# Two layers of long convolution and squared-ReLU MLP on one core: three kinds of DMA move to other places in SyncE's queue

## The chip, the core and the metric

The kernel runs on one core of a Trainium2 chip. The core has five engines with a queue of instructions each, worked off in order: TensorE (PE, with its weight loads shown as PEld), VectorE (DVE), ScalarE (ACT), GpSimd (POOL) and SyncE (SP). They tell each other through semaphores when a result is ready. SP computes nothing. It issues the kernel's DMAs, some 2,200 of them, in the order in which the program lists them, and an issue whose wait is not over holds up all that stand behind it. The metric is the device time of one execution in microseconds (us); lower is better.

## The reference, cut to what matters

With S = 2048 tokens, D = 1024 channels and F = 3584, two pairs of layers run one after the other:

```
x = x + A(layernorm(x));  x = x + B(layernorm(x))      # and both once more
A(q):  ks = short causal depthwise convolution of k (4 taps)
       kv = ks * v
       y  = causal convolution of kv with a filter as long as the sequence, per channel
       return q * (y + kv * ssm_D)
B(x):  r = max(x @ w1 + b1, 0);  return (r * r) @ w2 + b2
```

The convolution's result y does not depend on x, so it is computed once and used in both layers.

## The kernel before, in words

The MLP is the main work. The tokens are cut into 4 blocks of 512, and seven units (layer, block) run in turn; every matmul product is made of three passes (`mm3`, lines 355 to 358), since each operand is split into a high and a low part. A unit is a list of steps. A step takes one weight tile (`whl`, a high and a low half) and runs 12 matmuls of 512 columns. At the head of each step, `w_advance` issues the DMA of a weight tile 8 steps ahead into a raw buffer `wr` (lines 1099 and 1102), lets ACT make its high half (L1112) and DVE its low half (L1120). After the step's matmuls `w_store` writes some of the split weights to DRAM (L1128).

The convolution is laid between these steps. Channels are cut into 8 columns `c` of 128, and for each of the later token blocks `sb` = 1, 2, 3 three streams run:

- `fwd_x` (line 374) makes spectra of k*v: it loads `kT` and `vT` (L376, L378), forms the short convolution on ACT and DVE (L383, L386), multiplies by v (L388), transposes on PE (L441), transforms on PE (L412), adds on DVE (L423 to L428) and stores three tiles to `XD` (L433).
- `fwd_g` (line 450) makes spectra of the filter: it loads raw rows (L448) and the half that was carried over from the block before (`KD`, L457), transforms on PE (L475), copies on ACT (L480), combines on DVE (L485 to L490), stores the half to be carried (`KD`, L484), builds three tiles `go[1]`, `go[2]`, `go[0]` on DVE (L504, L505), one tick apart, and stores them to `GD` (L514). These tiles come from a ring of three buffers named `fg`, so the next column's raw rows take the place of `go[1]`. The two PSUM banks named `pt` are used by both streams and by the inverse transform (L616).
- `prod_stream` (line 540) multiplies the spectra. Its units (sb, group of 64 channels, one of three spectra pairs) are numbered 0 to 143, 48 for each sb and 6 for each column. A unit loads a tile from `XD` and one from `GD` (`load`, line 637: `cx` and `cg`, both on L646), POOL multiplies twice (L546), DVE sums each product two ticks later (L550), POOL folds (L696 to L701), PE transforms back (L616), ACT evicts (L622), SP stores to `YD` (L627).

A "tick" is one call of a stream's generator or one turn of a list of things due (`Later`). Several ticks can fall in one step. In sb = 1 a `cx` or `cg` tile holds two neighbouring units, two such tiles exist of each, and `fill` (line 649) calls for more loads after the second product of a unit: after an odd unit n for units n + 2 and n + 3, after the first unit of a column for the next two. Unit n is multiplied two ticks after its loads were called for, or later. With `sb` = 1 the stream often waits for the forward streams, and it catches up at one unit (two products) per step. The list that belongs to the steps (`slag`, among it L627 and the adds of L1729) is turned at a step's start, before `w_advance`; the products run after the step's matmuls, the forward streams behind them. So within one step SP gets, in this order: stores of L627, a weight load, a weight store, spectra loads, then the forward streams' DMAs.

Of the kernel before, what the change touches and what calls it, by code (L numbers as in the profile page):

```python
# [23 lines left out]
NB = S // T  # L24
# [4 lines left out]
BL = 256  # L29
NBL = S // BL  # L30
BT = T // BL
# [220 lines left out]
def tile_h3_mlp(ctx: ExitStack, tc: tile.TileContext, q, kT, vT, shk, ssmT, ssmD, w1, b1, w2, b2,  # L252
                fwd_t, pro_t, inv_t, sgn_t, out):
    nc = tc.nc
    V, A, G, PE, SY = nc.vector, nc.scalar, nc.gpsimd, nc.tensor, nc.sync
# [13 lines left out]
    KD = [[dram.tile([P, 2, BT * P], F32, name=f"kd{sb}_{c}") for c in range(KT)] for sb in range(NB - 1)]  # L269
# [14 lines left out]
    def mkfg(shape, dt=F32):  # L284
        return cv.tile(shape, dt, name="fg", bufs=3)

    def mkfk(shape, dt=F32):
        return cv.tile(shape, dt, name="fk", bufs=2)
# [62 lines left out]
    def give(*tiles):  # L351
        for o in tiles:
            held[slot.pop(id(o))[0]] = False

    def mm3(o, lh, ll, rh, rl, start, stop):
        PE.matmul(o, lh, rh, start=start, stop=False)  # L356
        PE.matmul(o, lh, rl, start=False, stop=False)  # L357
        PE.matmul(o, ll, rh, start=False, stop=stop)  # L358

    def hold(n):  # L360
        got = take(n)
        while not got:
            yield
            got = take(n)
        return got

    def dview(t, sb, c):
        return t[2 * c:2 * c + 2, :, BT * sb:BT * sb + BT].rearrange("g p b u -> p g b u")
# [77 lines left out]
    def load_g(raw, sb, c):  # L446
        for e in range(2):
            SY.dma_start(raw.rearrange("p (e b c) -> p e b c", e=2, b=BT)[:, e], g_rows(sb, c)[:, e])  # L448

    def fwd_g(sb, c):  # L450
        yield
        yield
        raw = mkfg([P, T])
        load_g(raw, sb, c)
        kk = [mkfk([P, 3 * BL]) for _ in range(2)]
        for r in range(2):
            SY.dma_start(kk[r][:, 0:BL], KD[sb - 1][c][:, r])  # L457
        for _ in range(FWD_WAIT):
            yield
        if sb > PLAIN:  # L460
            hi = mkfg([P, T], F32R)
            lo = mkfg([P, T], F32R)
            A.copy(hi, raw)
            yield
            V.tensor_sub(lo, raw, hi.bitcast(F32))
            yield
            yield
            yield
        oa = yield from hold(2)
        for r in range(2):  # L470
            ob = oa[r].rearrange("p (b e c) -> p e b c", b=BT, e=2)
            for e in range(2):
                q_ = slice(e * 256, e * 256 + 256)
                if sb <= PLAIN:
                    PE.matmul(ob[:, e], plain[0][:, 2 * e + r], raw[:, q_], start=True, stop=True)  # L475
                else:
                    mm3(ob[:, e], fh[:, 2 * e + r], fl[:, 2 * e + r], hi[:, q_], lo[:, q_], True, True)
        yield
        for r in range(2):
            A.copy(kk[r][:, BL:], oa[r])  # L480
        yield
        if sb < NB - 1:
            for r in range(2):
                SY.dma_start(KD[sb][c][:, r], kk[r][:, BT * BL:])  # L484
        V.scalar_tensor_tensor(kk[1][:, 0:T], kk[1][:, 0:T], sgn[:, 1:2], oa[0], op0=OP.mult, op1=OP.add)  # L485
        V.scalar_tensor_tensor(oa[1], kk[0][:, 0:T], sgn[:, 0:1], oa[1], op0=OP.mult, op1=OP.add)
        yield
        k0 = kk[1][:, 0:T]
        V.scalar_tensor_tensor(oa[0], oa[1], -1.0, k0, op0=OP.mult, op1=OP.subtract)
        V.tensor_sub(oa[1], oa[1], k0)  # L490
        yield
        odd = mkfg([P, T])
        parts = [t.rearrange("p (b e n) -> p e b n", b=BT, e=2) for t in (k0, oa[1], oa[0])]
        odds = [parts[0][:, 1]]
        for i in range(2):
            odds.append(odd[:, i * BL:i * BL + BL].rearrange("p (b n) -> p b n", b=BT))
            A.copy(odds[-1], parts[i + 1][:, 1])
        yield
        go = [None] * 3
        for i in (1, 2, 0):  # L500
            go[i] = mkfg([P, T])
            u = go[i].rearrange("p (g b u c) -> p u b g c", g=2, b=BT, u=2)
            ev, ov = (t.rearrange("p b (g c) -> p b g c", g=2) for t in (parts[i][:, 0], odds[i]))
            V.tensor_add(u[:, 0], ev, ov)  # L504
            V.tensor_sub(u[:, 1], ev, ov)  # L505
            yield
        if sb <= PLAIN:
            yield
            yield
        give(*oa)  # L510
        yield
        yield
        for i in range(3):
            SY.dma_start(dview(GD[i], sb, c), go[i].rearrange("p (g b u) -> p g b u", g=2, b=BT))  # L514
        yield

    plag, slag = Later(), Later()
    fwd_done = set()
# [2 lines left out]
    def fwd_stream(kind, fwd):  # L521
        for sb in range(1, NB):
            if sb > PLAIN:
                const_split()
            for c in range(KT):
                yield from fwd(sb, c)
                half_done[kind].add((sb, c))
                if all((sb, c) in d for d in half_done.values()):
                    plag.at(3, fwd_done.add, (sb, c))

    streams = [fwd_stream("x", fwd_x), fwd_stream("g", fwd_g)]

    def fwd_tick():
# [6 lines left out]
    def prod_stream():  # L540
        lag = plag
        sums, inv = [0, 0], [0, 0]

        def mult(st, xt, gt, j):
            pr = cv.tile([P, CU, j + 1], F32, name="cp", bufs=3)
            G.tensor_mul(pr.rearrange("p c i -> p i c"), xt[:, 0:j + 1], gt[:, j::-1])  # L546
            st["pr"] = pr
# [86 lines left out]
        got, when = {}, {}  # L634
        share = {}

        def load(n):
            sb, g, ty = units[n]
            nb = BT * sb + BT
            two = nb <= NBL // 2  # L640
            if n % 2 == 0 or not two:
                for nm in ("cx", "cg"):
                    share[nm] = cv.tile([P, 2 if two else 1, nb, CU], F32, name=nm, bufs=2)
            got[n] = [share[nm][:, n % 2 if two else 0] for nm in ("cx", "cg")]
            for t, src in zip(got[n], (XD[PAIRS[ty][0]], GD[PAIRS[ty][1]])):
                SY.dma_start(t, src[g, :, :nb])  # L646
            when[n] = lag.n

        def fill(n):
            sb = units[n][0]  # L650
            room = 3 if BT * sb + BT <= NBL // 2 and n % 2 else 2
            for m in range(n + 1, min(n + room + 1, len(units))):
                if m not in when:
                    if (units[m][0], units[m][1] // 2) not in fwd_done or (m > n + 2 and units[m][0] != sb):
                        return
                    load(m)

        pair = sm = None
        for n, (sb, g, ty) in enumerate(units):
            while n not in when:  # L660
                if (sb, g // 2) in fwd_done:
                    load(n)
                else:
                    lag.tick()
                    yield None
            while lag.n < when[n] + 2:
                lag.tick()
                yield None
            if ty == 0:
                while sums[0] - sums[1] >= 2:  # L670
                    lag.tick()
                    yield None
                sums[0] += 1
                sm = cv.tile([P, 3, BT, CU], F32, name="sm", bufs=2)
                if g % 2 == 0:
                    pair = {}
            for jj in range(BT):
                j = BT * sb + jj
                st = {"pair": pair}
                mult(st, *got[n], j)  # L680
                lag.at(2, red, st, sm, ty, jj)
                if jj == BT - 1:
                    if ty == 2:
                        lag.at(3, fin, st, sm, sb, g, 0)
                    fill(n)
                lag.tick()
                yield (j + 1) * CU * 1e-3
# [905 lines left out]
    lag = slag  # L1593
    xT = first_block()
    pds = prod_stream()
    ml = shut.enter_context(tc.tile_pool(name="ml", bufs=1, reuse_waits="tile"))
    def relu2(st, k):
# [544 lines left out]
    for sb in range(1, NB):  # L2142
        if WIN[sb] > lo_u:
# [3 lines left out]
            n = sum(last_step[u] + 1 - start_step[u] - 19 * (1 - PREP_PACE) for u in range(lo_u, hi_u))  # L2147
# [17 lines left out]
    for s, (k, u, c, a, i, tts, w) in enumerate(steps):  # L2165
# [79 lines left out]
        else:  # L2245
# [4 lines left out]
            r = rs[c, i]  # L2250
# [35 lines left out]
        if u + 1 < NU and not direct[u]:  # L2286
            n = s - start_step[u]
# [89 lines left out]
```

## Time and profile before

| what | us |
|---|---|
| median of 3 runs | 2678.66 (2674.75, 2678.66, 2678.91) |
| the profiled execution | 2673.35 |
| its span, first to last instruction | 2671.6 |
| PE busy | 2622.0 (98%) |
| DVE busy | 1977.1 (74%) |
| ACT busy | 1132.0 (42%) |
| POOL busy | 1044.2 (39%) |

"Busy" is the time in which an engine executes; issuing DMAs and waiting is not counted. The profile also gives the clock granted to TensorE in each stretch as a share of full speed, the chain of waits that ended last, the waits of each engine by what ended them, and a timeline of each engine.

### The profile page before, as it was taken

To read this page: it belongs to the slowest core of one execution; us is meant where nothing else is said; L and a number is where in the kernel's file an instruction comes from. 1 tells how busy PE (TensorE), PEld (TensorE's weight loads), DVE (VectorE), ACT (ScalarE), POOL (GpSimd) and SP (SyncE) were. 2 spreads that over 40 slices of the span, in tenths; PEclk is the share of its full clock that TensorE was granted. 3 is DMA by queue.
4 is the path that set the end of the run, shared out by engine and by line. 5 is a ranking of instruction groups with operands and counts; after the bars stand their busy time and mean duration, and the time that the engine had idled before them with its cause. 6 is when DMAs were issued, how large, how long until landed. Compare 5 with 4: busy or idle time off the path is not lost.

```text
span 2671.6 us, 36107 instructions
## 1 busy us (share of the span) xinstructions
PE 2622.0 (98%) x12388; PEld 2198.9 (82%) x12388; DVE 1977.1 (74%) x2845; ACT 1132.0 (42%) x1929; POOL 1044.2 (39%) x688
## 2 busy tenths in 40 slices
PE   8899999899999999999999999999999999999999
PEld 7888787788888888888888888888788778888887
DVE  7879888789887877779777765456778768777553
ACT  4454344434444333343333422345444575454442
POOL 2536665255642645427554275000100217536111
PEclk9999999999999999999999999999999999999999
DMA  8799898689989899788987888689888898878653
GB/s 253 245 322 316 296 309 280 229 298 377 344 294 318 313 337 302 268 304 302 339 303 251 307 293 301 209 260 320 305 298 304 268 332 256 265 249 312 233 195 119
DMA packets 380265, 763.16 MB, mean 286 GB/s; under 512 B 44064, under 2 KB 159408, under 8 KB 377008
## 3 DMA queue, kind: packets, MB, share of 16 engines
q1 hardware_dynamic: 380080, 760.85, 83.4%
q8 instruction: 98, 1.61, 0.2%
q14 instruction: 87, 0.71, 0.1%
HBM read 583.49 MB, written 177.21 MB: 285 GB/s over the span
## 4 chain that ended last, share of the span: by engine, by line
PE 83%; DMA 7%; DVE 5%; ACT 1%; issue 1%; POOL 1%; SPq 1%; DVEq 0%; ACTq 0%; POOLq 0%
PE p L356 24%; PE p L358 24%; PE p L357 24%; PE pt L356 2%; PE pt L358 2%; PE pt L357 2%; DMA whl<-wd_m 2%; PE p L1195 2%; DMA wr<-w 1%; DVE whl L1120 1%; DMA cg<-gd 1%; PE pt L475 0%; DMA yt<-yd 0%; PE pt L616 0%; PE pt L412 0%
## 5 line engine op out<-in xcount | busy, mean ns | idle before, releaser
L546 POOL TENSOR_TENSOR cp<-cx,cg 128x384 f32<-128x384 f32 (+5 forms) x288 | 542.2, 1896 | 566.2 <-DVE sm L550 371.0
L356 PE MATMUL p<-xh,whl 128*128 128x512 f32 (+1 forms) x1504 | 577.4, 384 | 3.1 <-DMA whl<-wd_m 2.2
L358 PE MATMUL p<-xh,whl 128*128 128x512 f32 (+1 forms) x1504 | 573.4, 381 | 3.3 <-DVE whl L1120 2.8
L357 PE MATMUL p<-xl,whl 128*128 128x512 f32 (+1 forms) x1504 | 573.2, 381 | 0.4 <-DVE xl L1517 0.4
L1112 ACT CAST whl<-wr 128x512 fp32r<-128x512 f32 x546 | 332.3, 619 | 467.8 <-PE p L358 282.2
L1120 DVE TENSOR_TENSOR whl<-wr,whl 128x512 fp32r<-128x512 f32 x486 | 427.6, 891 | 132.0 <-ACT whl L1112 131.0
L356 PE MATMUL p<-whl,rh 128*128 128x512 f32 x1204 | 476.0, 395 | 5.1 <-DVE fg L1718 2.9
L357 PE MATMUL p<-whl,rh 128*128 128x512 f32 x1204 | 471.1, 391 | 2.0 <-POOL whl L1120 1.2
L358 PE MATMUL p<-whl,rl 128*128 128x512 f32 x1204 | 470.6, 391 | 0.0
L358 PEld LDWEIGHTS p<-xh,whl 128*128 128x128 f32 x1504 | 283.7, 189 | 58.2 <-DVE whl L1120 3.0
L356 PEld LDWEIGHTS p<-xh,whl 128*128 128x128 f32 x1504 | 284.0, 189 | 57.6 <-issue 2.2
L357 PEld LDWEIGHTS p<-xl,whl 128*128 128x128 f32 x1504 | 283.8, 189 | 52.7 <-DVE xl L1517 0.6
L1609 DVE TENSOR_TENSOR rl<-wr,rh 128x512 fp32r<-128x512 f32 x140 | 143.0, 1022 | 179.2 <-ACT rh L1606 179.2
L1120 POOL TENSOR_TENSOR whl<-wr,whl 128x512 fp32r<-128x512 f32 x60 | 87.3, 1459 | 475.6 <-ACT whl L1112 457.4
L356 PEld LDWEIGHTS p<-whl,rh 128*128 128x128 f32 x1204 | 227.3, 189 | 53.8 <-DVE fg L1718 3.3
L357 PEld LDWEIGHTS p<-whl,rh 128*128 128x128 f32 x1204 | 227.2, 189 | 49.3 <-DVE whl L1120 2.4
L358 PEld LDWEIGHTS p<-whl,rl 128*128 128x128 f32 x1204 | 227.0, 189 | 47.9
L550 DVE TENSOR_REDUCE sm<-cp 128x128 f32<-128x384 f32 (+5 forms) x288 | 249.3, 874 | 8.9 <-POOL cp L546 8.9
L1601 ACT ACTIVATE wr<-p,b1t 128x512 f32<-128x512 f32 x138 | 95.3, 690 | 373.1 <-PE p L358 371.0
L1729 DVE TENSOR_TENSOR acc<-p,acc 128x512 f32<-128x512 f32 x152 | 100.0, 686 | 81.1 <-PE p L358 81.1
L696 POOL TENSOR_TENSOR sm<-sm 128x512 f32<-128x512 f32 x48 | 69.5, 1449 | 131.5 <-DVE sm L550 126.0
L356 PE MATMUL p<-whl,tq 128*128 128x512 f32 x276 | 107.4, 389 | 0.0
(394 smaller groups left out, 4281.7 us busy)
## 6 DMA issues: line engine op xcount, KB each, us to landing
whl<-wd_m SPq DMA_DIRECT2D x318, 512.0 KB, 5.5
wr<-w SPq DMA_DIRECT2D x442, 256.0 KB, 5.7
wd_m<-whl SPq DMA_DIRECT2D x70, 512.0 KB, 6.1
wr<-td SPq DMA_DIRECT2D x112, 256.0 KB, 5.0
cx<-xd SPq DMA_DIRECT2D x48, 512.0 KB, 5.8
cg<-gd SPq DMA_DIRECT2D x48, 512.0 KB, 6.7
tq<-hd SPq DMA_DIRECT2D x24, 1024.0 KB, 6.9
gd<-fg SPq DMA_DIRECT2D x72, 256.0 KB, 5.8
```

What stands on the lines that cost most here:

```text
L356: PE.matmul(o, lh, rh, start=start, stop=False)
L357: PE.matmul(o, lh, rl, start=False, stop=False)
L358: PE.matmul(o, ll, rh, start=False, stop=stop)
L546: G.tensor_mul(pr.rearrange("p c i -> p i c"), xt[:, 0:j + 1], gt[:, j::-1])
L550: V.tensor_reduce(sm[:, ty, jj], st["pr"], axis=AX.X, op=OP.add)
L696: E.tensor_add(s[:, 1:3], s[:, 1:3], s[:, 0:1].to_broadcast([P, 2, s.shape[2]]))
L1112: A.copy(t[:, 0], raws[n]["t"])
L1120: ENG[e[n % len(e)]].tensor_sub(t[:, 1], raws[n]["t"], t[:, 0].bitcast(F32))
L1195: PE.matmul(o, lh, r, start=start, stop=stop)
L1601: A.activation(r, st["o"], AF.Relu, bias=b1t[:, st["f"]:st["f"] + 1])
L1609: V.tensor_sub(st["lo"], st["r"]["t"], st["hi"].bitcast(F32))
L1729: V.tensor_add(accs[tt][:, d], o, accs[tt][:, d])
```

## The change

Three things are listed at other places of SP's queue. No instruction of another engine is added, removed or moved, and no DMA is added or removed.

1. The three stores of a column's filter spectra (L514) stood together. Now they are listed one tick apart, `go[1]` one tick earlier than before, `go[2]` where it was, `go[0]` one tick later. The column takes as many ticks as before.
2. The two stores of the carried half (L484) are listed two ticks later, after the DVE operations of L489 and L490.
3. The loads of spectra that `fill` calls for are listed one or two ticks later: for sb = 1 after the second tick, for sb = 2 and 3 after the first. The moment that counts for the earliest multiplication (`when`) stays that of the call.

```diff
@@ fwd_g
             A.copy(kk[r][:, BL:], oa[r])
         yield
-        if sb < NB - 1:
-            for r in range(2):
-                SY.dma_start(KD[sb][c][:, r], kk[r][:, BT * BL:])
         V.scalar_tensor_tensor(kk[1][:, 0:T], ...)
@@
         V.tensor_sub(oa[1], oa[1], k0)
         yield
+        if sb < NB - 1:
+            for r in range(2):
+                SY.dma_start(KD[sb][c][:, r], kk[r][:, BT * BL:])
         odd = mkfg([P, T])
@@
         give(*oa)
-        yield
-        yield
-        for i in range(3):
+        for i in (1, 2, 0):
+            yield
             SY.dma_start(dview(GD[i], sb, c), go[i].rearrange("p (g b u) -> p g b u", g=2, b=BT))
-        yield
@@ prod_stream: load, fill and the loop over units
-            when[n] = lag.n
@@
-                    load(m)
+                    when[m] = lag.n
+                    lag.at(2 if BT * sb + BT <= NBL // 2 else 1, load, m)
@@
                 if (sb, g // 2) in fwd_done:
+                    when[n] = lag.n
                     load(n)
```

## Rows read from the trace of the kernel before

**Rows 1.** The page: shares of the chain that ended last, by engine.
```profile
PE 83%; DMA 7%; DVE 5%; ACT 1%; issue 1%; POOL 1%; SPq 1%; DVEq 0%; ACTq 0%; POOLq 0%
```

**Rows 2.** Engines by stretch: start:end, length, busy of PE, PEld, DVE, ACT, POOL, clock, DMA share, GB/s.
```profile
120.00:530.00 410.00, 391.77 (x1975) 333.54 (x1974) 333.69 (x509) 179.27 (x319) 201.73 (x161) 0.98 0.87 291
680.00:1400.00 720.00, 719.47 (x3410) 604.24 (x3409) 575.92 (x782) 276.16 (x492) 347.68 (x192) 1.00 0.89 310
...
296.00:303.00 7.00, 4.25 (x12) 3.56 (x13) 7.00 (x11) 1.49 (x3) 3.50 (x4) 0.51 0.94 310
```

**Rows 3.** PE's timeline: start, length, instruction; in brackets idle time and its releaser.
```profile
298.75 1.10 PE L441 MATMUL pt<-ident,fx 128*128 128x128 f32 x4 [6.01 <-DVE fx L388]
...
442.84 1.97 PE L616 MATMUL pt<-sm,yh 128*128 128x128 f32 x8 [2.58 <-ACT whl L1112]
```

**Rows 4.** DVE's timeline, same columns, before the first stall.
```profile
285.00 0.55 DVE L550 TENSOR_REDUCE sm<-cp 128x128 f32<-128x384 f32 x1 [0.70 <-POOL cp L546]
...
290.38 3.67 DVE L386 SCALAR_TENSOR_TENSOR fx<-fx,shkt 128x512 f32<-128x512 f32 x3
...
297.93 0.68 DVE L388 TENSOR_TENSOR fx<-fx 128x512 f32<-128x512 f32 x1
```

**Rows 5.** DVE's timeline before the second stall.
```profile
416.85 0.69 DVE L1120 TENSOR_TENSOR whl<-wr,whl 128x512 fp32r<-128x512 f32 x1
419.00 0.55 DVE L550 TENSOR_REDUCE sm<-cp 128x128 f32<-128x384 f32 x1 [1.46 <-POOL cp L546]
...
442.29 0.41 DVE L505 TENSOR_TENSOR fg<-pt,fg 128x256 f32<-128x256 f32 x1
```

**Rows 6.** SP's waits from 120 to 480: line, releaser, us in total, times, longest.
```profile
SPq L514 <- DVE fg L505: 29.7, 8, 8.7
SPq L646 <- POOL cp L546: 11.6, 8, 3.5
SPq L484 <- ACT fk L480: 11.6, 5, 6.9
```

**Rows 7.** PE's waits from 454 to 496, same columns.
```profile
PE p L357 <- POOL whl L1120: 1.2, 2, 0.8
PE p L357 <- DVE whl L1120: 0.7, 2, 0.5
```

**Rows 8.** SP's timeline around the loads of units 13 to 15.
```profile
258.74 1.43 SPq L514 DMA_DIRECT2D gd<-fg  x3
...
260.75 0.77 SPq L646 DMA_DIRECT2D cx<-xd  x1
...
263.76 0.53 SPq L627 DMA_DIRECT2D yd<-wr  x1
264.38 0.57 SPq L1099 DMA_DIRECT2D wr<-w  x1
...
269.75 0.32 SPq L646 DMA_DIRECT2D cx<-xd  x1
```

**Rows 9.** SP's timeline around the loads of units 37 and 38.
```profile
410.43 0.43 SPq L646 DMA_DIRECT2D cx<-xd  x1
...
413.07 0.61 SPq L627 DMA_DIRECT2D yd<-wr  x1
413.80 0.63 SPq L1099 DMA_DIRECT2D wr<-w  x1
```

**Rows 10.** ACT's timeline: the evictions that L627 waits for.
```profile
263.14 0.38 ACT L622 ACTIVATE wr<-pt 128x256 f32<-128x256 f32 x1
...
412.62 0.38 ACT L622 ACTIVATE wr<-pt 128x256 f32<-128x256 f32 x1 [5.31 <-PE pt L616]
```

**Rows 11.** DMAs issued from 120 to 480: count, size, median us to landing.
```profile
cg<-gd SPq DMA_DIRECT2D x47, 256.0 KB, 5.3
```

**Rows 12.** POOL's timeline: the products of units 13 to 14 and 37 to 38.
```profile
267.11 3.24 POOL L546 TENSOR_TENSOR cp<-cx,cg 128x384 f32<-128x384 f32 x3 [8.67 <-DMA cg<-gd]
...
417.95 8.56 POOL L546 TENSOR_TENSOR cp<-cx,cg 128x384 f32<-128x384 f32 x6 [9.46 <-DMA cg<-gd]
```

**Rows 13.** DVE's waits from 120 to 480: line, releaser, us in total, times, longest.
```profile
DVE sm L550 <- POOL cp L546: 8.9, 14, 1.6
```

**Rows 14.** DVE's timeline: L386 while POOL stands idle (its next product starts at 405.52).
```profile
401.79 2.31 DVE L386 SCALAR_TENSOR_TENSOR fx<-fx,shkt 128x512 f32<-128x512 f32 x3
```

**Rows 15.** POOL's timeline: that pause, and the products beside the later L386.
```profile
293.47 3.99 POOL L546 TENSOR_TENSOR cp<-cx,cg 128x384 f32<-128x384 f32 x3
...
405.52 2.98 POOL L546 TENSOR_TENSOR cp<-cx,cg 128x384 f32<-128x384 f32 x2 [3.94 <-DMA cg<-gd]
```

## The prediction

> **What bounds the kernel now.** I read the chain that ended last first: 83% of it is PE [rows 1]. The reader is to see that anything else costs time only where PE stands still. The table by stretch says where that is. From 680 to 1400 PE is busy 719.47 of 720 us, although the streams that the change touches still run there; from 120 to 530 it is busy 391.77 of 410 [rows 2]. So the change can win or lose in those 410 us, while the spectra of block sb = 1 are made, and hardly elsewhere. PE's own timeline gives the two large holes: 6.01 us at 292 to 298.75 in front of the transposes L441, and 2.58 us at 440 to 442.84 in front of the inverse L616 [rows 3]. After the first the clock falls: 0.51 of full speed from 296 to 303, about the lower of the two levels (1.2 GHz), after PE had stood idle [rows 2]; PE then works 4.25 us at half speed, worth about 2.1 us.
>
> Both holes come from DVE running late. L441 starts at 298.75, 0.14 after L388 ends (297.93 + 0.68 = 298.61) [rows 3, 4]. For L616 the row names ACT, but L505's read of a `pt` bank ends at 442.29 + 0.41 = 442.70, again 0.14 before [rows 3, 5]; the bank is what L616 writes into, so I take DVE as the releaser. In the stretches that lead there (276 to 298, 417 to 442) DVE has no pause over 0.3 us except waits for POOL's products; all of these together in 120 to 480 are 14 waits, 8.9 us, none over 1.6 [rows 13]. 0.70 us lies ahead of L386 at 290.38, and 1.46 ahead of the run that ends in L505 [rows 4, 5]. So the question is whether POOL's products, and behind them the spectra loads, come earlier or later on DVE's queue.
>
> **The change part by part.** No compute instruction moves; the same DMAs are issued. What changes is what stands ahead of what on SP.
>
> *Filter stores one tick apart.* L514 waits 29.7 us for DVE in 8 cases of this stretch, since `go[0]`, the last made, is waited for five ticks after it was listed and then holds up everything [rows 6]. Now each tile has six ticks, and `go[1]`, whose buffer the next column's rows reuse, goes first. A step is about 2.6 us (12 matmuls at 719.47/3410 = 0.211 us each [rows 2], and the transforms between them), a tick at 1.4 a step about 1.9. So I expect at most 8 x 1.9 = 15 us of SP's waiting to go. *Carried halves two ticks later.* 11.6 us of waits for ACT, 5 times, go nearly all [rows 6]. *Spectra loads later.* The 11.6 us in which L646 waits for POOL to free a buffer go mostly too [rows 6].
>
> What is SP's time worth? PE waits for weights' low halves 1.2 + 0.7 us from 454 to 496, which a less blocked SP could bring sooner [rows 7]. Bounds: a gain of 1.9 us, or nothing, or a loss of the same size, if the stores, later now, push back other weights. I take a gain of 1. In the two holes weights are not what is late, so there the freed waits are worth nothing by themselves; they count only through the loads.
>
> *What the later loads cost.* In sb = 1 a load that was listed at the end of step s is now listed in step s + 1, since the stream does one unit (two products) per step there, or ends the step when it has to wait. The multiplication stays where it was, in step s + 2. The lead falls from two steps to one, 5.2 to 2.6 us, against 5.3 us from issue to landing [rows 11]; DVE's sum follows two ticks after the product and finds it unfinished. Worse, the load now stands behind whatever step s + 1 puts first on SP: the `YD` store L627, which waits for ACT's eviction, and a weight load.
>
> Hole at 298. The load of unit 13 was issued at 260.75 [rows 8]. It moves behind L627 (263.76) and L1099 (264.38 + 0.57 = 264.95). L627 can't leave before ACT's eviction ends, 263.14 + 0.38 = 263.52 [rows 10], which follows PE's pace; so a freer SP doesn't help. L627 0.53, L1099 0.57 and 0.2 between them: the load leaves at 264.8 instead of 260.75, 4 us later. Its product began at 267.11, the moment the second tile landed [rows 12]; it now begins near 270.8 and DVE waits about 1 us there. SP, which has the four issues of units 13 and 14 still to do, is then 2.9 us later for what follows, with unit 15's load at 269.75 [rows 8] now near 272.6. That product feeds DVE without slack, so the 1 grows to about 3. Against this stand the pauses in which SP catches up. Bounds: nothing (SP catches up, DVE's wait of 0.70 stays as it is [rows 4]) to the full 4.0 us. I take 3, nearer the end that the row of L627 sets. The hole grows from 6 to 9 us; the clock, already low for 296 to 303 [rows 2], may stay low another 3 us: 0 to 2 us, I take 0.7.
>
> Hole at 440. Unit 37's load was issued at 410.43 and moves behind L627 (413.07) and L1099 (413.80 + 0.63 = 414.43) [rows 9]; L627 is bound to ACT's eviction, 412.62 + 0.38 = 413.00 [rows 10]. So it leaves at 414.4, 4.0 us later. POOL sat idle 9.46 us for it, until 417.95 [rows 12], and DVE, done at 416.85 + 0.69 = 417.54, waited 1.46 us for the product [rows 5]. With the median landing [rows 11] instead of some 6.9 us for this one (its second tile left just after 410.43 + 0.43), the product begins 2.2 to 3.8 us later, and DVE's whole queue up to L505 with it. I take 3. Bounds: 0 to 4.0. Later units of this column don't take it back: they were not short of data.
>
> The other columns: their loads move too. PE has 410 - 391.77 - 6.01 - 2.58 = 9.6 us of idle left in this stretch [rows 2, 3], in small pieces, so DVE has some time in hand there; 0 to +3 for all together, I take +0.5.
>
> In sb = 2 and 3 the first tick comes right after the call, with nothing of SP between: no change of order. The stores' new places remain there, and PE has no idle time to lose: 0.
>
> Sum: -1 + 3 + 0.7 + 3 + 0.5 = +6.2 us. Against the profiled execution (span 2671.6, 1.75 of frame around it, 2673.35) that is 2679.6. The median of the runs lies 5.3 above the profiled one at 2678.66, so the forecast in its terms is 2678.66 + 6.2 = 2684.9, 0.23% slower. A measurement of this kernel can tell about 0.2% (5.4 us) from no change.
>
> On one point the Trainium skill speaks for another result. L386, three times over 512 elements with both inputs in SBUF, takes 2.31 us while POOL is idle until 405.52 and 3.67 us at 290.38, beside POOL's products from 293.47 [rows 4, 14, 15]. The Trainium skill, page "SBUF — State Buffer", section "Who interferes with whom", says that a DVE instruction with two SBUF inputs contends with a GpSimd one that reads SBUF, and the one that comes later blocks; the trace agrees, with these 1.4 us. That is the mechanism of rival 3 below.
>
> **The rivals.** *1. Faster: SP's freed waits win.* If SP gets so far ahead that loads leave no later than before in spite of their new place, DVE's waits for POOL shrink. Place: the two holes; price: the 0.70 and 1.46 us ahead of them go [rows 4, 5], the rest of rows 13 in part (about 2 us more), the weights' 1.9 [rows 7], and with a shorter first hole about 1 us of low clock. -7.1 us: 2671.6. It decides from the point at which the loads of units 13 and 37 leave by 261 and 411. For it: 30 + 12 + 12 us of SP's waits [rows 6]. Against it: L627, which follows PE [rows 8 to 10].
>
> *2. No change: the waits are hidden.* DVE's shift is taken up, since PE, late by one hole, gives the next column time, or SP catches up between; the gains in SP aren't on the path. 2678.7, within +-3. For it: only 18 us in 410 are idle at all [rows 2].
>
> *3. The later products step off DVE's late operations.* If POOL's products slide past L386 and L388, DVE gets back 1.4 us per L386 that runs alone [rows 4, 14], 2.8 in the two holes, about half of the loss: 2682.1, inside "no change". Against it: products sliding onto other two-input operations would cost as much.
>
> *4. The edit doesn't do what it says:* if the loads stay in the same step, the first two edits alone act: -2 us, 2676.7.
>
> **How the numbers follow.** Forecast 0.47 (its own range +2 to +13 us, with the bounds 4 + 4 + 2 + 3 at the top and 0 for one of the two holes at the bottom; of it 0.38 slower than 0.2%, 0.09 within). Rival 1: 0.24 (0.21 faster, 0.03 within). Rival 2: 0.15, of which 0.03 slower and 0.02 faster, since a run of small shifts can add up. Rival 3: 0.09 (0.03 slower). Rival 4: 0.05 (0.01 faster). Together: slower 0.44, within 0.2% 0.32, faster 0.24. For 8 in 10 the range runs from rival 1's middle with some of its tail, 2669, to the top of the bounds, 2695.
>
> **What would show it.** In the changed profile: L514's, L484's and L646's waits in this stretch at 15, 2 and 5 us or less; the load of unit 37 behind the weight load and its product about 3 us later against PE's steps; "DVE sm L550 <- POOL cp" at 15 us or more instead of 8.9; the two holes in front of L441 and L616 at about 9 and 5.5 us. Wrong if the holes shrink or vanish, if DVE's waits for POOL don't grow, or if PE gets idle time between 680 and 1400, which no step here provides.

## The result, and the profile after

| what | before | after |
|---|---|---|
| median of 7 runs, us | 2676.45 (2673.53 to 2678.91) | 2686.82 (2683.06 to 2692.41) |
| the profiled execution, us | 2673.35 | 2690.92 |
| its span, us | 2671.6 | 2689.1 |

The ratio is 1.0035, 95% interval 1.0024 to 1.0046: slower by 0.35%, or 9.4 us. The profiled execution before took 3.1 us less than its kernel's median, and the one after is the second slowest of its seven, 4.1 us above the median, so the two traces stand 17.5 us apart. They show where time is lost; how much an edit costs is taken from the ratios.

The page after: shares of the chain by engine (PE had 83% in [rows 1], DVE 5%):

```profile
PE 77%; DVE 8%; DMA 7%; POOL 2%; issue 2%; ACT 2%; SPq 1%; DVEq 0%; POOLq 0%; ACTq 0%
```

The table by stretch after, columns as in [rows 2]; the last line answers to its second, moved by the 10 us or more that the work there is later, the others are parts of its first:

```profile
225.00:268.00 43.00, 39.59 (x182) 33.49 (x183) 36.97 (x55) 20.14 (x37) 25.40 (x20) 0.95 0.84 286
268.00:315.00 47.00, 38.06 (x160) 31.24 (x160) 35.33 (x51) 15.04 (x29) 23.75 (x20) 0.90 0.81 272
420.00:470.00 50.00, 46.01 (x212) 38.65 (x212) 43.82 (x61) 22.33 (x41) 32.26 (x24) 0.93 0.81 256
690.00:1410.00 720.00, 719.47 (x3416) 604.52 (x3415) 575.46 (x780) 277.51 (x494) 348.89 (x194) 1.00 0.89 311
```

The same stretches of work before, for the first three lines:

```profile
221.00:260.00 39.00, 38.20 (x186) 32.26 (x184) 35.91 (x52) 19.70 (x35) 24.35 (x19) 1.00 0.92 316
260.00:301.00 41.00, 34.99 (x162) 29.32 (x161) 34.89 (x51) 15.58 (x29) 22.26 (x20) 0.94 0.99 326
406.00:450.00 44.00, 41.42 (x197) 34.85 (x196) 39.90 (x55) 20.17 (x36) 28.93 (x22) 0.96 0.80 261
```

From 690 to 1410 PE is as busy as it was, 719.47 of 720. Nearly all is lost in block sb = 1, and two things are to be seen there. PE stands still for longer: 3.41 + 8.94 + 3.99 us in the three stretches, before 0.80 + 6.01 + 2.58. And it works more slowly, for the clock is lower: 39.59 / 182 = 0.218 us per matmul against 0.205, 0.238 against 0.216, 0.217 against 0.210; times 182, 160 and 212 matmuls that is 2.2 + 3.5 + 1.4 = 7.1 us. (The third stretch holds 212 matmuls after and 197 before, so its 1.4 is rougher than the others.)

PE's timeline after, the five holes over 1 us in these columns; the fourth answers to the first of [rows 3], the fifth to its second:

```profile
226.43 1.10 PE L441 MATMUL pt<-ident,fx 128*128 128x128 f32 x4 [3.28 <-DVE fx L388]
...
266.50 0.94 PE L441 MATMUL pt<-ident,fx 128*128 128x128 f32 x4 [1.98 <-DVE fx L388]
...
300.37 0.47 PE L356 MATMUL p<-whl,rh 128*128 128x512 f32 x1 [2.63 <-ACT whl L1111]
312.15 1.10 PE L441 MATMUL pt<-ident,fx 128*128 128x128 f32 x4 [6.31 <-DVE fx L388]
...
458.83 2.04 PE L614 MATMUL pt<-sm,yh 128*128 128x128 f32 x8 [3.57 <-DVE fg L505]
```

(L616, L550, L546, L627, L1099 and L646 are L614, L548, L544, L625, L1098 and L644 after, L514 is L513, L484 is L491.) PE's program is the same in both kernels, so one can subtract the starts of the same L441 in the two traces: what PE has lost by then.

| L441 before, us | 92.61 | 164.95 | 221.93 | 259.47 | 298.75 | 340.10 | 405.45 | 449.04 | 717.04 |
|---|---|---|---|---|---|---|---|---|---|
| after minus before | -1.15 | +1.07 | +4.50 | +7.03 | +13.40 | +14.11 | +14.99 | +17.18 | +17.90 |

The first step, 2.2 us between 93 and 165, has no new hole. It is clock that was lower from 93 to 100 and from 114 to 121, ahead of the products, in this execution and in some of the experiments'. I count it to no edit. The rest, 16.4 us, falls into the columns between 165 and 470.

DVE's waits after, from 120 to 490, answering to [rows 13]; then SP's, answering to [rows 6]:

```profile
DVE sm L548 <- POOL cp L544: 26.7, 18, 5.5
```

```profile
SPq L513 <- DVE fg L505: 19.0, 12, 4.1
...
SPq L644 <- POOL cp L544: 14.7, 7, 3.9
...
SPq L491 <- ACT fk L480: 5.5, 1, 5.5
```

DVE's wait for products has tripled, from 8.9 us to 26.7. SP waits less for L505 and L480 and, against the forecast, no less for L544 (11.6 us before). I read this as a freer SP that comes to the loads sooner and waits there: with the stores alone moved (experiment 2) the wait for L544 is 16.4 us.

### The profile page after: what moved, and what is told of

It is laid out like the page before. It is cut to its first block, busy times and chain, and to the rows that moved or that the text cites. A ratio compares the mean times of both kernels' runs of the same rounds, so it can differ in the third digit from the quotient of the medians.

```text
span 2689.1 us, 36158 instructions
## 1 busy us (share of the span) xinstructions
PE 2629.7 (98%) x12388; PEld 2205.0 (82%) x12388; DVE 1983.9 (74%) x2845; ACT 1133.1 (42%) x1929; POOL 1045.5 (39%) x688
## 4 chain that ended last, share of the span: by engine, by line
PE 77%; DVE 8%; DMA 7%; POOL 2%; issue 2%; ACT 2%; SPq 1%; DVEq 0%; POOLq 0%; ACTq 0%
PE p L358 22%; PE p L356 22%; PE p L357 22%; PE pt L358 2%; PE pt L356 2%; PE pt L357 2%; PE p L1194 2%; DMA cg<-gd 1%; DVE whl L1119 1%; DMA wr<-w 1%; DMA whl<-wd_m 1%; POOL cp L544 1%; DVE sm L548 1%; DMA wd_m<-whl 1%; DMA xd<-fy 1%
## 5 line engine op out<-in xcount | busy, mean ns | idle before, releaser
L544 POOL TENSOR_TENSOR cp<-cx,cg 128x384 f32<-128x384 f32 (+5 forms) x288 | 543.1, 1898 | 587.2 <-DVE sm L548 367.6
L548 DVE TENSOR_REDUCE sm<-cp 128x128 f32<-128x384 f32 (+5 forms) x288 | 249.3, 873 | 26.7 <-POOL cp L544 26.7
```

The costliest lines, as they stand in the source:

```text
L548: V.tensor_reduce(sm[:, ty, jj], st["pr"], axis=AX.X, op=OP.add)
```

## The experiments

Theory: edit 3 puts loads behind a step's other issues, so products and DVE are late. Against it: that the stores' new places cost the time; that too little lead of the products costs it rather than the loads' place; that DVE is short of time in this block whatever the loads do. All ratios are to the kernel before; each interval is in brackets.

**1. The loads alone.** The kernel before with edit 3 (the last three hunks of the diff).

> The kernel before with the third edit alone (spectra loads listed one or two ticks later; both kinds of stores where they were). Theory (the loads' later place makes POOL's products late, DVE waits for them, and PE waits for DVE in front of the transposes and the inverse): as slow as the whole change or slower, +6 to +16 us against before; DVE's waits for POOL's products from 120 to 490 us grow from 8.9 to 20 us or more; the idle time in front of L441 stays at 10 us or more. Rival A (the stores' new places cost the time, for instance because go[0] is stored one tick later): within 0.2% of before, and those waits stay below 12 us.

Measured: 2692.88 us, 1.0058 [1.0044, 1.0072]. DVE's and PE's waits from 120 to 490 (L550 and L616 as before):

```profile
DVE sm L550 <- POOL cp L546: 26.1, 19, 5.3
```

```profile
PE pt L441 <- DVE fx L388: 12.8, 5, 6.3
PE pt L616 <- DVE fg L505: 3.6, 1, 3.6
```

They are close to those of the whole change (26.7, 12.3 and 3.6 us). So the loads carry the loss, and more than all of it.

**2. The stores alone.** The kernel before with edits 1 and 2 (the first three hunks).

> The kernel before with the first two edits alone (filter stores one tick apart, carried halves two ticks later; loads where they were). Theory: -5 to +2 us against before, since the freed waits of SP lie beside PE's work; SP's wait for L505 falls from 29.7 to 20 us or less, DVE's waits for POOL's products stay at 5 to 11 us. Rival A (the stores cost it): +5 us or more.

Measured: 2673.27 us, 0.9988 [0.9979, 0.9997]. PE's timeline has the two old holes, smaller (6.01 and 2.58 in [rows 3]):

```profile
295.28 1.10 PE L441 MATMUL pt<-ident,fx 128*128 128x128 f32 x4 [4.94 <-DVE fx L388]
...
439.14 1.13 PE L614 MATMUL pt<-sm,yh 128*128 128x128 f32 x8 [1.79 <-DVE fg L505]
```

The stores gain 0.12%, about 3 us; the gain is small beside its interval. By the code, edit 3 with one tick instead of two would leave every engine's queue in the order of this kernel, so what costs should be the second tick, which takes a load into the next step; a kernel with one tick was not run.

**3. Only the farthest loads later.** The whole change, but in sb = 1 only the load of unit n + 3 is deferred by two ticks.

```
-  lag.at(2 if BT * sb + BT <= NBL // 2 else 1, load, m)
+  lag.at(2 if BT * sb + BT <= NBL // 2 and m == n + 3 else 1, load, m)
```

> The whole change, but in sb = 1 only the load of unit n + 3 (a new tile, which waits until POOL has freed the buffer, and which is multiplied three units later) moves two ticks; units n + 1 and n + 2 are loaded where they were. Theory (what costs is a lead cut from two steps to one, and only the near units are that near): no slower than the stores alone, -5 to +2 us against before, DVE's waits for POOL's products below 13 us. Rival B (any spectra load that moves behind the next step's stores and weight loads costs): +5 us or more, waits of 18 us or more.

Measured: 2673.19 us, 0.9985 [0.9976, 0.9993], as good as experiment 2 and faster than both kernels. DVE's wait:

```profile
DVE sm L548 <- POOL cp L544: 8.0, 15, 1.6
```

The load of n + 3 moves behind the next step's stores and weight loads like the others and costs nothing, so that place alone is not what costs (rival B). Unit n + 3 has two units to be multiplied ahead of it; units n + 1 and n + 2 have none or one, and by the experiments below those can't be late.

**4. The products later too.** The whole change, and the products of sb = 1 two ticks later, so that their lead over the loads is that of before.

```
-  when[m] = lag.n
+  when[m] = lag.n + 2 * (BT * sb + BT <= NBL // 2)
```

> The whole change, but in sb = 1 the earliest multiplication moves two ticks with the load, so that the lead of two ticks is back and the products come later on all engines' queues. Theory (the lost lead is the cost): DVE's waits for POOL's products fall back to 12 us or less and the time is within 0.2% of before or better, unless the later products collide elsewhere. Rival C (the DMAs' order alone costs, whatever DVE waits for, by late weights): +5 us or more with PE waiting for weights.

Measured: 2686.02 us, 1.0031 [1.0019, 1.0042]: a miss. DVE's waits did fall, not to 12 us, and new ones came. DVE's and PE's from 120 to 490:

```profile
DVE sm L548 <- POOL cp L544: 14.7, 10, 2.7
```

```profile
PE p L357 <- DVE whl L1119: 5.4, 3, 2.4
PE pt L441 <- DVE fx L388: 4.0, 2, 3.4
```

It moves work on every engine, so its time does not separate lead from place. PE's waits for weights with a loss over 5 us are the sign that was named for rival C, so this run by itself speaks for C. As the cause of the whole change C is not supported: there PE waits 2.6 + 0.2 us for weights, and in experiment 3, with the DMAs' order changed too, nothing is lost.

**5. Only the first loads of a column later.** Edits 1 and 2, and of edit 3 in sb = 1 only the loads called for after an even unit (at a column's start: units 13 and 37, among others).

```
-  lag.at(2 if BT * sb + BT <= NBL // 2 else 1, load, m)
+  lag.at(2 if BT * sb + BT <= NBL // 2 and n % 2 == 0 else 1, load, m)
```

> Both edits of the stores, and of the loads only those that the first unit of a column calls for in sb = 1 move two ticks (units 13, 14, 37, 38 and their like); all others stay. Theory, with the prediction's account of the hole at 440: those loads stand behind the YD store and the next weight load, so the idle time in front of the inverse is 3 to 4.5 us as in the whole change (3.6) and not 1.8 as with the stores alone; the hole of 3.3 us in the third column, where a load from within a column moved, is gone (under 1 us); time +1 to +6 us against the stores alone. Rival D (the inner loads carry all of the loss): no more idle time at the inverse than 2 us, time within 2 us of the stores alone.

Measured: 2676.12 us, 1.0005 [0.9996, 1.0015]. PE's holes, and DVE's waits for units 13 and 37:

```profile
300.07 1.10 PE L441 MATMUL pt<-ident,fx 128*128 128x128 f32 x4 [7.87 <-DVE fx L388]
...
444.81 2.05 PE L614 MATMUL pt<-sm,yh 128*128 128x128 f32 x8 [3.68 <-DVE fg L505]
```

```profile
270.81 0.55 DVE L548 TENSOR_REDUCE sm<-cp 128x128 f32<-128x384 f32 x1 [0.92 <-POOL cp L544]
...
421.39 0.55 DVE L548 TENSOR_REDUCE sm<-cp 128x128 f32<-128x384 f32 x1 [2.99 <-POOL cp L544]
```

Against experiment 2 the holes are 2.93 and 1.89 us longer, and DVE waits 0.92 us where it did not for unit 13, 2.99 instead of 1.10 for unit 37. This is the prediction's account of both holes: +3 forecast for each. For the first the path can be followed too. PE is 1.45 us later than in experiment 2 by then (the start of L441 ahead of it); less that, unit 13's load leaves 4.45 us later, and unit 15's, not moved itself, 2.74 (forecast 4 and 2.9). DVE waits 0.92 us for unit 13, where it had not waited, and 1.90 instead of 0.31 for unit 17: 2.51 of the 2.93. The second hole is overestimated by a third. The two moves cost 1.0005 - 0.9988 = 0.17%, about 4.5 us, uncertain by 0.13%.

**6. Only the near loads inside a column later.** Edits 1 and 2, and of edit 3 the loads of unit n + 2 after an odd n.

```
-  lag.at(2 if BT * sb + BT <= NBL // 2 else 1, load, m)
+  lag.at(2 if BT * sb + BT <= NBL // 2 and n % 2 and m < n + 3 else 1, load, m)
```

> Both edits of the stores, and of the loads only the near ones called for inside a column move two ticks (units n + 1 and n + 2 after an odd unit n); the first unit's and the far ones stay. Theory: the hole in front of L441 in the third column is back (2.5 us or more, unit 5's load), DVE's waits for POOL's products from 120 to 490 are 14 to 24 us, time +3 to +9 us against the stores alone. Rival E (only loads behind the YD store cost): that hole stays under 1 us and the time within 2 us of the stores alone.

Measured: 2693.72 us, 1.0059 [1.0045, 1.0074], more than expected and more than the whole change. Waits from 120 to 490:

```profile
PE pt L441 <- DVE fx L388: 19.8, 5, 7.9
```

```profile
SPq L644 <- POOL cp L544: 38.2, 15, 5.5
```

The near loads hurt, and the hole of the third column is there (6.16 us, up to 226.21). The size is hardly theirs alone: the load of n + 3 is now listed ahead of that of n + 2, and n + 2 shares its new buffer instead of the half that was free in the older one. SP waits 38.2 us for POOL to free buffers, against 14.7 in the whole change. The cleaner price is a difference: the whole change less experiment 5, 1.0035 - 1.0005 = 0.30%, about 8 us for the inner loads, if the parts add up. Of these, by experiment 3, the far ones cost nothing when they move alone. No run moves the near inner loads alone with the buffers used as before.

**7 and 8. The transposes two ticks later.** L441 stands four ticks behind L388 in sb = 1; here six, in the kernel before (7) and in that of experiment 3 (8).

```
-  for _ in range(4 if sb == 1 else 7):
+  for _ in range(6 if sb == 1 else 7):
```

> The kernel before, with two more ticks in sb = 1 between the product with v on DVE (L388) and the transposes on PE (L441). Theory (PE's holes there are DVE's lateness and nothing else): the idle time in front of L441 from 120 to 500 us falls from 6.8 to under 1 us, the time by 4 to 9 us. Rival F (DVE is short of time as a whole in this stretch, so the hole moves to the next thing that PE waits for): the idle time of PE from 120 to 500 stays at 10 us or more, time within 0.2% of before. The x stream gets longer by two ticks a column, which can make the products of sb = 1 some 20 us later.

> The stores' edits, the far loads alone two ticks later, and two more ticks between L388 and L441 in sb = 1: the version that the runs so far point to. Theory: the gains add up, -6 to -14 us against before. Rival F: -2 to -6 us, no better than without the two ticks.

Measured: 2705.59 us, 1.0108 [1.0093, 1.0123], and 2697.39 us, 1.0081 [1.0068, 1.0095]: both miss. The holes before L441 go, so L388 was what they waited for, but PE's waits turn up elsewhere. Experiment 7, PE's waits from 300 to 500 and its busy time from 690 to 1410:

```profile
PE p L357 <- DVE whl L1120: 5.3, 2, 4.9
```

```profile
690.00:1410.00 720.00, 709.77 (x3348) 594.69 (x3347) 571.60 (x775) 270.54 (x482) 337.98 (x189) 1.00 0.88 307
```

Two ticks more for every column seem to push work into the later blocks: from 690 to 1410 PE now stands idle for 10.23 us, before 0.53. A hole's releaser says who is late, not that the waiter should go later.

**9 and 10. Each store edit alone,** in the kernel before: the filter stores one tick apart (9), the carried halves two ticks later (10).

> The kernel before with edit 1 alone: the three filter stores one tick apart, go[1], go[2], go[0]; carried halves and loads as before. The two store edits together gave 0.9988 [0.9979, 0.9997], and in their trace SP waited 12.1 us for L505 instead of 29.7, PE 6.0 us for L388 instead of 6.8 and 1.8 us for L505 instead of 2.6. Theory: the gain comes from this edit, since L514's wait, up to 8.7 us long, is what stood ahead of the loads of units 13 and 15 to 17; expected ratio 0.998 to 0.9995, SP's wait for L505 at 12 to 17 us, the hole at 298 below 5.5 us. Rival: the carried halves' waits (11.6 us) are what held the loads; then this kernel is within 0.05% of before and the hole at 298 stays at 6 us.

> The kernel before with edit 2 alone: the stores of the carried half two ticks later; filter stores and loads as before. Theory (the filter stores carry the gain): ratio 0.9995 to 1.0005, SP's wait for L480 falls from 11.6 to about 8 us, its wait for L505 stays at 25 to 35 us, and the holes at 298 and 440 stay at about 6 and 2.6 us. Rival (the carried halves carry it): ratio 0.998 to 0.9993 and a hole at 298 below 5.5 us.

Measured: 0.9991 [0.9982, 1.0000] and 0.9997 [0.9988, 1.0005]. The hole at 298 in experiment 9; in 10 it is 6.07 us:

```profile
296.21 1.10 PE L441 MATMUL pt<-ident,fx 128*128 128x128 f32 x4 [4.96 <-DVE fx L388]
```

By the holes the gain is the filter stores'; by the times the two edits can't be told apart.

## Why the prediction was right, and where it was not

The forecast, +6.2 us, has the sign and the mechanism: loads behind a step's other issues, late products, late DVE, PE standing still. That the sum came within 3.2 us of the measured 9.4 is luck: the two holes that it was built on gave less than forecast, the stores gained more, and the term put at 0.5 us carries most of the loss.

**Stores, forecast -1.** Measured -3 us (experiment 2). The gain came by another way than forecast: PE's weights were as late as before, but the two holes shrank by 1.1 and 0.8 us. Ahead of the first, unit 17's load left 1.4 us sooner against PE (273.39 instead of 277.20, PE being 2.40 us ahead) and DVE's wait for it fell from 0.70 us to 0.31; ahead of the second, unit 37's load left no sooner, but landed faster, and DVE waited 1.10 us instead of 1.46. That is rival 1's mechanism, on a small scale, for the stores alone. In the whole change the waits named as its sign did not all fall: L513's is 19.0, not 15, L491's 5.5, not 2, and L644's 14.7, not 5.

**Hole at 298, forecast +3.** The load went where the prediction put it, right behind L627's store and the weight load. SP's timeline after:

```profile
270.80 0.52 SPq L625 DMA_DIRECT2D yd<-wr  x1
271.41 0.58 SPq L1098 DMA_DIRECT2D wr<-w  x1
272.04 0.43 SPq L644 DMA_DIRECT2D cx<-xd  x1
```

With the column-start loads alone the term measures +2.93 us (experiment 5). In the whole change the hole is 0.30 longer than before, or 1.37 longer than with the stores alone. PE had stood still at 226, 266 and 300 already, so I take it that part of DVE's lateness showed there instead: lost sooner, not saved.

**Hole at 440, forecast +3.** Measured +1.89 (experiment 5 against 2) and +0.99 (after against before; +1.78 against experiment 2). Unit 37's load went behind L627's store, but ahead of the weight load; SP's timeline, and the product on POOL, answering to [rows 9, 12]:

```profile
428.02 0.53 SPq L625 DMA_DIRECT2D yd<-wr  x1
428.59 0.63 SPq L644 DMA_DIRECT2D cx<-xd  x1
...
430.75 0.38 SPq L1098 DMA_DIRECT2D wr<-w  x1
```

```profile
433.94 8.57 POOL L544 TENSOR_TENSOR cp<-cx,cg 128x384 f32<-128x384 f32 x6 [10.46 <-DMA cg<-gd]
```

Less the 14.99 us that PE is late there, the load leaves at 413.60, 3.17 us later than before, not 4.0, and the product begins at 418.95, 1.00 us later. From the start of the `cx` issue to the product it took 5.35 us instead of 7.52, and this took back 2.17 us; the prediction had allowed for 0.2 to 1.8. It comes with the new place and is no accident of one trace: experiments 1 and 5, with the load in the new place, took 5.44 and 5.88 us, and experiments 2, 3, 6, 9 and 10, with it in the old one, 6.75 to 7.83. In the old place a weight load had left 1.5 to 1.9 us ahead, in the new one 4.8 to 5.2; that this is the reason is not shown.

**Other columns, forecast +0.5: the term that failed.** The nearest measure is the inner loads' +8 us (whole change less experiment 5), clock included; it also holds what inner loads add in the two columns above. The step took PE's idle time, in small pieces, as a sign that DVE has time in hand there, and put the loss at nearly nothing. PE's idle time does not tell that. In the third column DVE has 0.49 us in hand: L388 ended at 220.59 + 0.85 = 221.44, and the third column's L441 started at 221.93, without idle time. DVE's timeline before:

```profile
213.42 0.55 DVE L550 TENSOR_REDUCE sm<-cp 128x128 f32<-128x384 f32 x1 [0.32 <-POOL cp L546]
...
220.59 0.85 DVE L388 TENSOR_TENSOR fx<-fx 128x512 f32<-128x512 f32 x1
```

But the load of unit 5, the product of that first row, moves by more than the two that the prediction followed. SP's timeline after:

```profile
207.15 0.85 SPq L376 DMA_DIRECT2D fx<-kT  x1
...
208.58 0.38 SPq L1098 DMA_DIRECT2D wr<-w  x1
...
210.98 0.33 SPq L644 DMA_DIRECT2D cx<-xd  x1
```

Before it left at 204.84, ahead of L376. Less PE's 1.07 it is 5.07 us later: the forward streams' loads at the step's end and the weight DMAs at the next one's head now go first. Then SP waits for the landing of a store to `XD` (its waits from 209 to 211.5):

```profile
SPq L644 <- DMA xd<-fy: 1.5, 1, 1.5
```

The load had not waited for that store in its old place; why it does here is not shown. DVE's timeline after, from that product to L388:

```profile
218.32 0.55 DVE L548 TENSOR_REDUCE sm<-cp 128x128 f32<-128x384 f32 x1 [1.91 <-POOL cp L544]
...
221.26 3.62 DVE L386 SCALAR_TENSOR_TENSOR fx<-fx,shkt 128x512 f32<-128x512 f32 x3
...
225.47 0.82 DVE L388 TENSOR_TENSOR fx<-fx 128x512 f32<-128x512 f32 x1
```

Less PE's 1.07, L548 is 3.83 us later than before. Less the 0.49 in hand that makes 3.34, and the new hole is 3.28. The same kind of load is that of unit 17, called for after unit 15: DVE waits 4.91 us for it instead of the 0.70 of [rows 4]. That wait, not the one for unit 13, stands ahead of the hole at 312. The hole at 300 is a late weight: ACT's cast ends at 299.68 + 0.61 = 300.29, behind three operations of the step before, and ACT had waited 2.69 us for raw weights at 294.74. No run takes it apart from the rest.

**Clock, forecast +0.7.** In the profiled execution 7.1 us of PE's time, by the stretches above. The forecast charged one dip, the old one, made longer; but the new holes have their own. The 7 us from the end of the holes at 226, 266, 312 and 459:

```profile
226.00:233.00 7.00, 6.57 (x29) 5.69 (x30) 7.00 (x11) 2.81 (x5) 2.58 (x2) 0.77 0.62 226
...
266.00:273.00 7.00, 6.50 (x28) 5.54 (x29) 5.71 (x10) 4.13 (x8) 0.00 (x0) 0.76 0.43 142
...
312.00:319.00 7.00, 6.85 (x25) 5.78 (x26) 5.71 (x10) 1.49 (x3) 4.34 (x3) 0.57 0.77 243
...
459.00:466.00 7.00, 7.00 (x26) 6.00 (x27) 6.96 (x13) 0.85 (x2) 4.04 (x3) 0.59 0.58 175
```

1.00 is 2.4 GHz, and a mean between 0.5 and 1 a mixture of it and 1.2 GHz. In the 7 us after each of these the clock is 1.00 again. Before, the first two places, with holes under 1 us, were at 1.00; the last two were at 0.64 and 0.76, after shorter holes. The dip does not grow with the hole: in experiment 5 the 7 us from 300 on, behind a hole of 7.87 us, are at 0.72. Nor does 7.1 us hold for the median, which is 9.4 us longer and not 17.5: if the idle time is the same 6.95 us in other executions, which no trace shows, the clock's share there is some 2.5 us, an estimate.

**No loss from 680 on, forecast 0.** Right: 719.47 of 720 us busy again, and the lag of PE grows by 0.7 us after 449.

**Rivals.** 2 (hidden) and 4 (the loads stay in their step) fall with the result and with experiments 1 and 2. 1 holds for the stores alone. 3 did not come about as forecast: L386 still takes 3.62 us beside POOL's work at 221.26, as long as the 3.67 of [rows 4], and not the 2.31 of [rows 14]. The Trainium skill, page "SBUF — State Buffer", section "Who interferes with whom", says that a DVE instruction with two SBUF inputs contends with a GpSimd one reading SBUF. The trace agrees, by that 1.3 us. But the prediction named the wrong work of POOL: beside the L386 of [rows 4] run its folds, L696 to L701, from 289.95 to 293.50, and the product of [rows 15] only at its end. POOL's timeline before, and the L386 ahead of the hole at 266 on DVE, before and after:

```profile
289.95 1.29 POOL L696 TENSOR_TENSOR sm<-sm 128x512 f32<-128x512 f32 x1 [3.72 <-DVE sm L550]
```

```profile
253.33 2.80 DVE L386 SCALAR_TENSOR_TENSOR fx<-fx,shkt 128x512 f32<-128x512 f32 x3
...
260.74 4.34 DVE L386 SCALAR_TENSOR_TENSOR fx<-fx,shkt 128x512 f32<-128x512 f32 x3
```

Here DVE, late, did slide: L386 onto a product of POOL's (261.38, before 255.57) and 1.54 us longer, L504 and L505 behind it off it, 0.41 us each instead of 1.24 and 1.50. From the start of L386 to the end of L388 it is 5.61 us instead of 5.99, so both ways together cost nothing, as the prediction's objection to rival 3 said.

The accounts in times: stores -3, column-start loads +4.5, inner loads +8, together +9.5 against +9.4 measured. That they add up follows from how they were taken, as differences of ratios in a row, and each difference is uncertain by some 0.15%, 4 us. Experiment 1 is an independent look: without the stores' edits the loads cost 0.58%, with them 1.0035 - 0.9988 = 0.47%, the same within the intervals.

## What to carry to other kernels

When a load is listed later in an in-order queue, follow each one by itself and write down what it is passed by: an issue with a wait, or a block of issues at a loop's head, costs more than the ticks suggest. Compare the lead that is left with the time from issue to landing, and defer only loads that still have work in hand ahead of them (here two units). Charge each new hole in TensorE of the size seen here (2 to 6 us) with a stretch of lower clock behind it. And don't take idle time of one engine as slack of another.

## What the runs showed of the hardware

In the profiled execution the lower clock behind the holes cost as much as the holes: 7.1 us, against 16.34 - 9.39 = 6.95 us of more idle time in the same three stretches. A load listed later landed faster: unit 37's two tiles were ready for POOL 5.35 to 5.88 us after the first issue in three traces with the new place (after, experiments 1 and 5), and 6.75 to 7.83 us in six with the old one. L386 on DVE took 2.31 us while POOL was idle 3.62 beside its folds, and 4.34 beside its folds and a product. And the clock dipped between 93 and 121 us by different amounts in executions with the same PE order there, worth 2.2 us; what decides it was not found.
